# Attention beside a state-space convolution: 14 of 16 normalising multiplications on GpSimd, and two small transfers of the gate held back

## The chip, the cores and the metric

The kernel runs on one NeuronCore of a Trainium2 chip. The metric is the device time of one execution in microseconds, the median of several runs. The engines are TensorE (PE in the profile), VectorE (DVE), ScalarE (ACT), GpSimd (POOL) and SyncE (SP); GpSimd and SyncE issue most of the transfers.

## The reference

Two branches are computed from inputs of 2048 rows by 448 columns in bf16, and a gate mixes them.

```
g = sigmoid((x * gate_w).sum(-1))                  # one number per row
a = softmax(q k^T / sqrt(28)) v, then @ wo         # 16 heads of 28, one shared k and v
K[d, l] = Re sum_n C[d,n] exp(dt[d] A[d,n] l) dt[d] B[d,n]     # 256 modes, complex
b = causal convolution of u with K along the rows, rounded to bf16, + u * Dskip
out = g * a + (1 - g) * b                          # b is called with u = x
```

## The kernel before, in words

**Attention.** The 16 units are the four query chunks of 512 rows times the four groups of four heads. A unit has 64 score tiles (16 key tiles times four heads) of 128 x 512 in PSUM; 1024 tiles in all are taken in turn three and two at a time, as 410 sets. For each set TensorE multiplies `qT` or its copy `qM` with `kT` (L1422, L456, L1456; near the end L1444), ScalarE takes the exponential of the whole set in one instruction (L1497), and TensorE adds `expT` times `vaug` into `psB` (L1518). A column of ones in `vaug` gives the softmax's denominators.

At the end of each of the first 15 units, `norm(i)` does the following. VectorE copies `psB` to `acc` (L1210; `acc` has two halves, used in turn). GpSimd sends the denominators to the small tile `denT`. VectorE takes reciprocals (L1216) and, from unit 12 on, multiplies them by the gate (L1218). GpSimd sends them to the DRAM buffer `R_scratch` and reads them back, spread over partitions, into `rdenB` with four transfers. At last `onT = acc * rdenB` is computed: 128 x 512 elements, two f32 operands in SBUF, a bf16 result (L1222). The sixteenth unit has a path of its own (`scaled`). After units 3, 7 and 11, `outp` multiplies `onT` by `Wo` (L1190) and VectorE adds the result into `O` (L1201); the last chunk has `early` and `last`.

`qproj(i + 2)` prepares the query projections of a unit two units ahead, with VectorE's L933 and L939, and four transfers of GpSimd copy `qT` to `qM`.

**Convolution.** There are 14 blocks `c` of 32 channels. VectorE builds a table of powers for each: `masters` (L968 to L988), `tables` (L1025, L1040, L1044, L1048, L1054, L1058, and at its end the negation L1061). GpSimd contributes two small copies per block (L1011, L1013). TensorE turns a table into the convolution's kernel (`kgen`, L1084), VectorE copies this to `kstg` (L1096), transfers write it to `KP_scratch`, SyncE loads it back in Toeplitz form into ring buffers (`tload`), and TensorE convolves (`conv`, L1151), with VectorE's L1161 and L1181 at the end of each of 28 halves.

**The gate.** `g` is computed at the start into the tile `gt` (L769 to L773). Two transfers on GpSimd's queue then send 512 single f32 values to `RG_scratch` (`gw`, L774) and read them back in another layout (`gr`, L776), which L1218 needs in units 12 to 14.

**Order.** Nothing is written in final order. `Prog.op` and `Prog.dma` record operations with engine, estimated time, priority `pr` and dependences, and `schedule` plays them through: at each step it takes the operation that can start first, by (earliest start, `pr`, number). So every engine's order is fixed when the program is built, and an estimate that changes at one place moves instructions of all engines behind it. While it runs, each engine follows its order and waits on semaphores. One estimate belongs to GpSimd and VectorE together: a GpSimd operation of 500 ns or more is taken to hold VectorE up for `PORT` = 0.55 of its time (L356, L357). Where TensorE would be idle, the plan inserts a filler matmul (L1403).

Of the kernel before, what the change touches and what calls it, by code (L numbers as in the profile page):

```python
# [7 lines left out]
ALU = mybir.AluOpType  # L8
# [4 lines left out]
P = 128  # L13
# [29 lines left out]
XQ = NT * 512  # L43
QS = 4 * D + 64
GATE = (30, 35)
XDVE = ((1, 0), (1, 1), (1, 2))
WARM = 64
HELD = ((27, 3), (27, 9), (27, 15), (27, 21))
# [40 lines left out]
def dram(t, off, dims):  # L89
    return bass.AP(tensor=t.tensor, offset=t.offset + off, ap=[list(d) for d in dims])  # L90
# [7 lines left out]
class Prog:  # L98
# [101 lines left out]
    def schedule(self):  # L200
# [17 lines left out]
        free = {e: 0.0 for e in ENG}  # L218
# [18 lines left out]
        while done < n:  # L237
            best = None
            for e in ENG:
                T = free[e]  # L240
                for i in ready[e]:
                    o = ops[i]
                    r = max(rt[i], T)
                    if o.lock is not None:
# [3 lines left out]
                        r = max(r, L[1] + (300.0 if o.pr >= 2 else 0.0))  # L248
                    for k in o.comm or ():
                        if k in comm:  # L250
                            r = max(r, ops[comm[k]].end)
                    if o.psb == 3:
                        if not opened:
                            continue
                        for x in ready["pe"]:
                            if ops[x].pr <= 0.0 and r < rt[x] < r + o.ns - self.NEAR:
                                r = max(rt[x], T) + ops[x].ns
                    if e == "pe":
                        j = (npe + o.ni - self.FIRST - 1) // self.BLOCK + 1
                        if j < len(block):  # L260
                            r = max(r, block[j])
                            if o.pr >= 1 and block[-1] > r:
                                left = self.FIRST + (len(block) - 2) * self.BLOCK - npe - o.ni
                                r = max(r, block[-1] - left / self.NEED)
                    if o.slot is not None and o.slot[0] == "T" and self.spaced[0] < r < self.spaced[1]:
                        r = max(r, lastT + self.GAP)
# [5 lines left out]
            o = ops[i]  # L272
            spare = [x for x in locks if x[0] is None and x[1] <= free[e]]
            if e == "pe" and (opened or spare) and r > self.FWIN and self.filler is not None and npe > self.FIRST + self.BLOCK:
# [5 lines left out]
                if r - T >= w and busy < self.FLOW * self.FWIN and (j >= len(block) or block[j] <= T):  # L280
                    b = 6 if opened else spare[0][3]
                    o = self.op("pe", lambda x, b=b: self.filler(x, b), self.FILL, rd=["one", "id"], ni=2)
# [7 lines left out]
                    i, r = o.i, T  # L290
                    ready[e].append(i)
            ready[e].remove(i)
            if e == "pe" and o.mode != mode:
                r = max(r, free[e] + self.SWITCH)
# [35 lines left out]
            if o.slot is not None:  # L330
                free[e] = r + o.iss * o.ndma
                s = r if e == "pool" else max(r, dmafree)
                end = max(s + o.ns, free[e]) + self.DMA_NS + o.extra
                if e == "pool" and o.ns >= self.PUSHES:
                    for x in flight:
                        x[1] = max(x[1], r)
                        if x[2] > r:
                            x[2] += self.PUSH * o.ns
                            t = x[2] + self.DMA_NS + x[0].extra
                            if t > x[0].end:  # L340
                                x[0].end = t
                                for j in succ[x[0].i]:
                                    rt[j] = max(rt[j], t + self.SEM_NS + (self.LATE if ops[j].pr in self.LAZY and r < 360000.0 else 0.0))
                    flight = [x for x in flight if x[2] > r]
                if o.slot[0] == "T":
                    flight.append([o, s, max(s + o.ns, free[e])])
                if o.ns > 1000.0 and e == "sp":
                    self.moving = [x for x in self.moving if x[1] > r - 20000.0] + [(r, end)]
                dmafree = max(dmafree, s) + o.ns
            else:  # L350
                ns = o.ns
                if e == "pe" and self.HALF[0] < r < self.HALF[1]:
                    ns *= self.HALF[2]
                free[e] = r + ns
                end = free[e] + o.lat
                if e == "pool" and o.ns >= 500.0:  # L356
                    free["dve"] = max(free["dve"], r) + self.PORT * o.ns  # L357
            o.end = end
            if o.unlock is not None:
                L = [x for x in locks if x[0] is o.unlock][0]  # L360
# [88 lines left out]
def el(n, rate=0.96, fix=68):  # L449
    return fix + n / rate  # L450
# [23 lines left out]
class Kernel:  # L474
# [205 lines left out]
    def prep_x(self):  # L680
# [6 lines left out]
        for q in range(4):  # L687
            for hp in range(2):
# [14 lines left out]
                key = ("xT", hp, q)  # L703
                if (hp, q) not in XDVE:
                    pg.op("act", lambda e, d=dst, s=src: e.activation(d, s, AF.Copy), 1000, rd=[("b", b)], wr=[key])
# [498 lines left out]
    def norm(self, i):  # L1204
        pg = self.pg
        g = i % 4
        ao = 512 * (i % 2)
        av = self.acc.v(0, P, ao, [[1, 512]])
        ov = self.onT.v(0, P, 512 * g, [[1, 512]])
        pg.op("dve", lambda e: e.tensor_copy(av, self.psB.v(0, P, 0, [[1, 512]])), el(512), rd=[("b", 6)], wr=[("acc", i % 2)], pr=0)  # L1210
        dv = self.denT.v(0, P, 0, [[1, 16]])
        if True:
            rs = self.acc.rs
            pg.dma([(dv, bass.AP(tensor=self.acc.h, offset=28 * rs + ao, ap=[[32 * rs, 4], [16, 32], [1, 16]]))],
                   (128, 64), "dn", rd=[("acc", i % 2)], wr=["dn"], pr=0, eng="pool", extra=5000)
            pg.op("dve", lambda e: e.reciprocal(dv, dv), 163, rd=["dn"], wr=["dn"], pr=2)  # L1216
            if i >= 12:
                pg.op("dve", lambda e: e.tensor_tensor(dv, dv, self.gt.v(0, P, 32, [[1, 16]]), ALU.mult), 80, rd=["dn", "gT"], wr=["dn"], pr=2)  # L1218
            pg.dma([(dram(self.R, i * 2048, [[16, P], [1, 16]]), dv)], (128, 64), "rw", rd=["dn"], wr=[("R", i)], pr=0, eng="pool", extra=4500)
            pg.dma([(self.rdenB.v(32 * h, 32, 0, [[1, 512]]), dram(self.R, i * 2048 + 512 * h, [[0, 32], [1, 512]])) for h in range(4)],  # L1220
                   (128, 2048), "rdb", rd=[("R", i)], wr=["rd"], pr=0, eng="pool", extra=5500 if i < 14 else 1000)
            pg.op("dve", lambda e: e.tensor_tensor(ov, av, self.rdenB.v(0, P, 0, [[1, 512]]), ALU.mult),  # L1222
                  el(512), rd=[("acc", i % 2), "rd", "onw"], wr=[("on", g)], pr=2)

    def tailmats(self):
        pg = self.pg
# [148 lines left out]
    def main(self):  # L1375
        pg = self.pg
# [31 lines left out]
        def qk(s):  # L1408
# [42 lines left out]
            def full(e, t, b):  # L1451
                if t >= NLAST:
                    part(e, t, b, 0, False)
                    return part(e, t, b, 1, False)
                i, kt, h = dec(t)
                return e.matmul(self.psS.v(0, P, 512 * b, [[1, 512]]), kT.v(0, P, 128 * kt, [[1, 128]]),  # L1456
                                self.qM.v(0, P, (i % 2) * XQ + 512 * h, [[1, 512]]),
                                start=True, stop=True, tile_position=(0, 0), skip_group_check=True)
            if s < 8 or len(ts) == 3 or s >= 14 and (ts[0] % 64 < NEWQ or s >= ROWS):
                rd = set()  # L1460
                for t in ts:
                    i, kt, h = dec(t)
                    rd |= {("q", i % 2), ("kT", (kt if t < NLAST else declast(t)[1]) // 4)}
                o = pg.op("pe", row, 220, rd=sorted(rd, key=str), wr=bk, pr=0, mode="q", ni=2 * len(ts))
# [3 lines left out]
            else:  # L1468
                for t, b in zip(ts, bs):
                    i, kt, h = dec(t)  # L1470
                    kt = kt if t < NLAST else declast(t)[1]
                    o = pg.op("pe", lambda e, t=t, b=b: full(e, t, b), 220, rd=[("qM", i % 2), ("kT", kt // 4)],
                              wr=[("b", b)], pr=0, mode="f", ni=2)
            if s in GATE:
                pg.after[self.gate[GATE.index(s)]] = o.i
            if s < WARM and ts[0] % 64 < 52 and (ts[0] < 64 or ts[0] % 64 > 14):
# [16 lines left out]
            for t in ts:  # L1493
# [3 lines left out]
            o = pg.op("act", lambda e: e.activation(expT.v(0, P, 512 * es[0], spread(es, n)),  # L1497
                                                self.psS.v(0, P, 512 * bs[0], spread(bs, n)),
                                                AF.Exp, scale=SQ), 63.5 + 426.5 * n, rd=bk, wr=ew, pr=0)
            self.lastexp = o.i  # L1500

        def pv(v):
            ts = range(4 * v, 4 * v + 4)
# [35 lines left out]
        for s in range(len(sets)):  # L1539
            qk(s)  # L1540
            last = sets[s][-1]
            if s >= 2:
                while nv < NTL // 4 and 4 * nv + 3 <= sets[s - 2][-1]:
                    pv(nv)
                    nv += 1
                    if nv % 64 == 0 and nv // 64 < 4:
                        for tt in range(4):
                            self.outp(nv // 64 - 1, tt)
            for t in sets[s]:
                if t % 64 == 63 and t // 64 + 2 < 16:  # L1550
                    self.qproj(t // 64 + 2)
# [68 lines left out]
```

## Time and profile before

| | |
|---|---|
| median of 3 runs (range) | 496.68 us (496.52 to 496.79) |
| the profiled execution: its own time / span | 499.2 / 497.2 us |
| granted TensorE clock | 0.997 |
| VectorE's multiplication L1222 | 15 times, 682 ns each |
| GpSimd's copies L1011 / L1013 | 14 each, mean 1025 / 692 ns |
| `qM` transfers, median from issue to landing | 4.6 us |
| `RG_scratch` write / read back, issue to landing | 10.8 / 4.4 us |

The span goes from the first instruction to the last; the execution's own time is measured from outside and is 2.0 us longer. It lies 2.5 us over the median of the runs that were timed without a profile.

### The profile page before, as it was taken

Reading aid. Unit: us, or ns where it says so; the run is one execution under the profiler, and the core shown is the slowest. Engines: PE = TensorE matmul, PEld = TensorE weight load, DVE = VectorE, ACT = ScalarE, POOL = GpSimd, SP = SyncE. Lnnn points to the kernel's source line nnn. Section 1 sums busy time; section 2 is a strip of 40 time slices with the busy share of each in tenths; the row PEclk is TensorE's granted clock in tenths of the full one; section 3 lists DMA queues with packets and bytes.
Section 4 is the critical chain, followed back from the end, with each engine's and each line's share of the span. In section 5 each row is a group of like instructions: output and inputs, shape, how many; then the busy total and the mean of one; then the engine's idle time right before and its main releaser. Section 6 shows DMA issues by size and latency. Waiting matters only on the chain.

```text
span 497.2 us, 17393 instructions
## 1 busy us (share of the span) xinstructions
PE 476.1 (96%) x7657; PEld 218.4 (44%) x7657; DVE 456.3 (92%) x847; ACT 482.2 (97%) x433; POOL 220.4 (44%) x390
## 2 busy tenths in 40 slices
PE   8889999999999999999999999999999999999897
PEld 6423233353443435444443434444434354545443
DVE  6999999999999999999999999999999999993334
ACT  6989999999999999999999999999999999999995
POOL 8415034225243435767339376653764433431110
PEclk9989999999999999999999999999999999999999
DMA  8945012916719267873924956688393759595932
GB/s 254 269 57 112 1 34 57 343 45 178 229 18 337 69 188 219 227 211 94 309 68 100 323 163 139 179 227 205 114 238 112 225 145 290 196 279 159 284 105 70
DMA packets 91767, 85.44 MB, mean 172 GB/s; under 512 B 24970, under 2 KB 86716, under 8 KB 91692
## 3 DMA queue, kind: packets, MB, share of 16 engines
q1 hardware_dynamic: 80794, 72.49, 49.9%
q0 software_dynamic: 10624, 11.70, 10.6%
q8 instruction: 60, 0.98, 0.8%
q14 instruction: 15, 0.12, 0.1%
q10 hardware_dynamic: 274, 0.14, 0.1%
HBM read 76.36 MB, written 5.23 MB: 164 GB/s over the span
## 4 chain that ended last, share of the span: by engine, by line
DVE 55%; ACT 32%; PE 9%; DMA 2%; issue 1%; POOL 0%
ACT expT L1497 32%; DVE tab L1025 16%; DVE tab L1040 9%; DVE tab L1054 4%; DVE msq L968 3%; DVE tmp L1048 3%; DVE kstg L1096 2%; DMA qM<-qT 2%; DVE cst L1161 2%; DVE mbf L988 2%; DVE T L972 2%; DVE T L970 2%; DVE qT L933 1%; DVE qT L939 1%; DVE acc L1210 1%
## 5 line engine op out<-in xcount | busy, mean ns | idle before, releaser
L1497 ACT ACTIVATE expT<-psS 128x1536 bf16<-128x1536 f32 (+1 forms) x410 | 464.9, 1332 | 4.1 <-PE psS L1456 2.1
L1025 DVE TENSOR_TENSOR tab<-tab,mbf 128x512 bf16<-128x512 bf16 (+4 forms) x140 | 139.7, 1001 | 0.0
L456 PE MATMUL psS<-qT,kT 32*128 32x512 bf16 x713 | 101.2, 379 | 7.8 <-ACT expT L1497 4.9
L1518 PE MATMUL psB<-expT,vaug 128*32 128x512 bf16 x1000 | 100.2, 390 | 0.1
L170 POOL DMA_DIRECT2D KP_scratch<-kstg x104 | 57.9, 563 | 72.5 <-DVE kstg L1096 71.8
L1040 DVE TENSOR_TENSOR tab<-tab 128x256 bf16<-128x256 bf16 (+4 forms) x140 | 77.7, 575 | 0.0
L1456 PE MATMUL psS<-qM,kT 128*128 128x512 bf16 x240 | 72.8, 385 | 2.8 <-DMA qM<-qT 1.8
L1518 PEld LDWEIGHTS psB<-expT,vaug 128*32 128x32 bf16 x1000 | 25.6, 93 | 77.2 <-issue 72.6
L170 POOL DMA_DIRECT2D qM<-qT x64 | 32.6, 518 | 44.0 <-DVE qT L939 18.9
L170 POOL DMA_DIRECT2D U<-in_A_x_dram x60 | 39.7, 666 | 24.0 <-PE psS L1151 10.6
L1403 PE MATMUL psB<-ident,one 128*128 128x512 bf16 x155 | 49.4, 384 | 0.0
L1437 PEld LDWEIGHTS <-kT 32*128 32x128 bf16 x713 | 24.9, 91 | 47.4 <-issue 37.2
L170 POOL DMA_DIRECT2D rdenB<-R_scratch x60 | 30.6, 517 | 32.1 <-DMA R_scratch<-denT 32.0
L1151 PE MATMUL psX<-T,U 128*26 128x128 bf16 (+3 forms) x1792 | 42.8, 226 | 0.8 <-issue 0.8
L1151 PEld LDWEIGHTS psX<-T,U 128*26 128x26 bf16 (+3 forms) x1792 | 36.7, 138 | 14.1 <-issue 10.9
L1151 PE MATMUL psS<-T,U 128*26 128x128 bf16 (+3 forms) x1600 | 39.2, 227 | 0.9 <-issue 0.7
L1151 PEld LDWEIGHTS psS<-T,U 128*26 128x26 bf16 (+3 forms) x1600 | 32.4, 138 | 13.6 <-issue 10.0
L1054 DVE TENSOR_TENSOR tab<-tab,tmp 128x1984 bf16<-128x1984 bf16 x28 | 32.3, 1184 | 0.1
L1048 DVE TENSOR_TENSOR tmp<-tmp,mq 128x64 bf16<-128x64 bf16 (+4 forms) x70 | 25.6, 365 | 0.4
L968 DVE TENSOR_TENSOR msq<-T 128x512 f32<-128x512 f32 (+1 forms) x40 | 24.8, 620 | 0.0
L1456 PEld LDWEIGHTS psS<-qM,kT 128*128 128x128 bf16 x240 | 15.0, 98 | 21.1 <-ACT expT L1497 14.8
L170 POOL DMA_DIRECT2D R_scratch<-denT x15 | 8.6, 571 | 34.4 <-DVE denT L1216 14.0
(198 smaller groups left out, 543.2 us busy)
## 6 DMA issues: line engine op xcount, KB each, us to landing
T<-KP_scratch SPq DMA_DIRECT2D x212, 272.0 KB, 5.2
rdenB<-R_scratch POOLq DMA_DIRECT2D x60, 64.0 KB, 3.1
U<-KP_scratch SPq DMA_DIRECT2D x12, 272.0 KB, 5.5
U<-in_A_x_dram SPq DMA_DIRECT2D x20, 112.0 KB, 4.4
qM<-qT POOLq DMA_DIRECT2D x64, 32.0 KB, 4.6
tab<-in_A_x_dram SPq DMA_DIRECT2D x4, 448.0 KB, 5.4
KP_scratch<-kstg POOLq DMA_DIRECT2D x104, 16.0 KB, 2.4
xT<-XS_scratch POOLq DMA_DIRECT2D x3, 448.0 KB, 4.8
```

What stands on the lines that cost most here:

```text
L170: return [e.dma_start(o, i, **kw) for o, i in pairs]
L456: return e.add_instruction(mybir.InstMatmult(start_tensor_calc=True, stop_tensor_calc=True, tile_size=(32, 128), tile_position=pos, bass_s ...
L968: pg.op("dve", lambda e: e.tensor_tensor(m2(msq), z2, z2, ALU.mult), el(2 * n), rd=[kr, ki] + first, wr=["msq"], pr=pr)
L1025: mul = lambda e, o, a, b: e.tensor_tensor(o, a, b, ALU.mult)
L1040: vo(lambda e, dv=dv, tv=tv, k=k: e.tensor_tensor(dv, dv, tv, ALU.add if k else ALU.subtract), n, [kt[k], kd[k]], [kd[k]], 1.92 if lv else ...
L1048: vo(lambda e, w=w, lv=lv: e.tensor_tensor(rho.v(0, P, (32 - 2 * w) * 2, [[64, 32], [2, w], [1, 2]]), rho.v(0, P, (32 - w) * 2, [[64, 32], ...
L1054: vo(lambda e, k=k: e.tensor_tensor(tab.v(0, P, FM + k * FP + 2, [[64, 32], [2, 31], [1, 2]]), tab.v(0, P, lm + k * PL + 62, [[64, 32], [- ...
L1151: r = e.matmul(ps.v(32 * j, 32 - m0, 128 * k, [[1, 128]]), self.U.v(0, P, (4 * gi + j) % UA // UC * UW + (2 * m0 + par) * UC + (4 * gi + j ...
L1403: return e.matmul(t.v(0, P, off, [[1, 512]]), self.one.v(0, P, 2, [[0, P]]), self.ident.v(0, P, 0, [[0, 4], [1, P]]), start=b != 6, stop=b ...
L1456: return e.matmul(self.psS.v(0, P, 512 * b, [[1, 512]]), kT.v(0, P, 128 * kt, [[1, 128]]), self.qM.v(0, P, (i % 2) * XQ + 512 * h, [[1, 51 ...
L1497: o = pg.op("act", lambda e: e.activation(expT.v(0, P, 512 * es[0], spread(es, n)), self.psS.v(0, P, 512 * bs[0], spread(bs, n)), AF.Exp, ...
L1518: r = e.matmul(self.psB.v(32 * h, 32, 0, [[1, 512]]), vaug.v(0, P, 32 * kt, [[1, 32]]), expT.v(0, P, 512 * ring[t], [[1, 512]]), start=(kt ...
```

## The change

Three edits:

- In `norm`, the multiplication of units 0 to 13 is put on GpSimd instead of VectorE, with an estimate of 2200 ns and priority 2.1. Unit 14 stays on VectorE.
- In `schedule`, an operation with priority 2.1 is exempt from the `PORT` estimate: the plan takes it to cost VectorE nothing.
- In `main`, the first of the gate's transfers (`gw`) gets a dependence on the exponential of set 24 (counted from 0). The second one waits for the first, as before.

```diff
+GATEOUT = 24
...
                 if e == "pool" and o.ns >= 500.0:
-                    free["dve"] = max(free["dve"], r) + self.PORT * o.ns
+                    free["dve"] = max(free["dve"], r) + (0.0 if o.pr == 2.1 else self.PORT * o.ns)
...
-            pg.op("dve", lambda e: e.tensor_tensor(ov, av, self.rdenB.v(0, P, 0, [[1, 512]]), ALU.mult),
-                  el(512), rd=[("acc", i % 2), "rd", "onw"], wr=[("on", g)], pr=2)
+            far = i < 14
+            pg.op("pool" if far else "dve", lambda e: e.tensor_tensor(ov, av, self.rdenB.v(0, P, 0, [[1, 512]]), ALU.mult),
+                  2200.0 if far else el(512), rd=[("acc", i % 2), "rd", "onw"], wr=[("on", g)], pr=2.1 if far else 2)
...
             self.lastexp = o.i
+            if s == GATEOUT:
+                self.gw.deps[o.i] = 1
```

The instructions themselves stay the same in kind and number, apart from the engine of the 14 multiplications and from fillers, of which the new order has 8 more (170 instead of 162). ScalarE's order is unchanged. The orders of TensorE and VectorE are the same up to the first multiplication, near 85 us, and differ from there on.

## The prediction

> **What bounds the kernel now.** I read the page first (busy shares, slices, the chain), then the idle gaps of ScalarE, then the stages, and last the places where VectorE and GpSimd meet. Busy time, and the costliest groups of ScalarE and VectorE:
>
> ```profile
> PE 476.1 (96%) x7657; PEld 218.4 (44%) x7657; DVE 456.3 (92%) x847; ACT 482.2 (97%) x433; POOL 220.4 (44%) x390
> ...
> DVE 55%; ACT 32%; PE 9%; DMA 2%; issue 1%; POOL 0%
> ...
> L1497 ACT ACTIVATE expT<-psS 128x1536 bf16<-128x1536 f32 (+1 forms) x410 | 464.9, 1332 | 4.1 <-PE psS L1456 2.1
> ```
>
> ScalarE's 410 exponentials (L1497) run nearly end to end from 21.8 to 490.75 us and stood idle only 4.1 us before one of them. That is all that a faster supply could win in the stream. Yet the chain runs 55% over VectorE: ScalarE is only just the slower of two.
>
> The stages show the second one:
>
> ```profile
> 150.00:200.00 50.00, 49.26 (x796) 22.04 (x794) 50.00 (x88) 50.00 (x45) 22.31 (x39) 1.00 0.65 199
> 250.00:300.00 50.00, 48.65 (x697) 20.59 (x694) 50.00 (x85) 49.91 (x45) 31.16 (x50) 1.00 0.60 162
> 350.00:400.00 50.00, 47.60 (x821) 21.26 (x817) 50.00 (x91) 50.00 (x46) 26.07 (x46) 1.00 0.68 187
> 450.00:498.00 48.00, 41.97 (x925) 22.69 (x923) 15.04 (x30) 41.22 (x38) 5.22 (x10) 1.00 0.48 145
> ```
>
> (busy us of PE, PEld, DVE, ACT, POOL, then clock, DMA share, GB/s.) VectorE has no free moment until about 457 us, when its fourteenth table is done, and then almost nothing. So VectorE's work up to that table has a delivery date. TensorE takes each table in a fixed place of its order (L1084), after the negation L1061. In the timeline that handover leaves 0.2 to 0.8 us in nine of 14 tables and 1.26 us in the last (450.49 to 451.75), and TensorE waits for almost none of them.
>
> The largest gaps of ScalarE are at the start:
>
> ```profile
> 34.22 1.02 ACT L1497 ACTIVATE expT<-psS 128x1024 bf16<-128x1024 f32 x1 [1.30 <-PE psS L1456]
> 36.05 1.45 ACT L1497 ACTIVATE expT<-psS 128x1536 bf16<-128x1536 f32 x1 [0.81 <-PE psS L1422]
> ...
> 24.99 0.79 POOL L170 DMA_DIRECT2D RG_scratch<-gt  x1 [1.22 <-DVE gt L772]
> 27.54 0.30 POOL L1011 COPY tab<-mbf 128x128 bf16<-128x128 bf16 x1 [1.76 <-DVE mbf L988]
> 36.12 0.71 POOL L170 DMA_DIRECT2D gt<-RG_scratch  x1 [8.29 <-DMA RG_scratch<-gt]
> ```
>
> Four gaps between 32.91 and 38.90 us sum to 1.30 + 0.81 + 0.19 + 0.18 = 2.5 us. TensorE waits 1.8 us for the copy qM, which takes 10.1 us to land where the next takes 2.7. In those microseconds the gate's 512 four-byte elements are under way (landing in 10.8 us), and SP's issues of U, mostly 0.63 us, stretch to 4.80 us at 29.11.
>
> **The change, part by part.** *Gate transfers.* They leave the first 36 us and wait for exponential 24 (start 52.36 us, so about 53.9). Behind the first of them on GpSimd's queue stand denT of unit 0 (sent at 56.63 before), then the second transfer, then qM of unit 2, sent at 66.10 and first needed at tile 128, near 84 us. Even a landing of 10.8 us again ends at about 66, so this costs nothing; without that cover a late qM would cost its lateness. At the start the gain lies between 0 (the jam is U's own) and 2.5 us. I take 2.5, because jam and transfer coincide.
>
> *Off VectorE.* A multiplication L1222 takes 682 ns, 0.60 from its start to the next start. Thirteen stand before the last negation (the thirteenth at 435.9, the fourteenth at 462.7): 13 x 0.60 = 7.8 us. In the new order one qT cast (0.60) and the two small denT operations (0.24 + 0.18) also come later and one O addition (0.41) earlier, 0.6 us net. So VectorE has 8.4 us less to do before the last table.
>
> *What the order asks for.* The built program counts on that. The plan is told that these 14 cost VectorE nothing while they run, and places TensorE's table multiplications earlier among the score tiles: table 13 behind tile 923 instead of 943, table 10 behind 765 instead of 783. A tile is 464.9 / 1024 = 0.454 us of ScalarE, so table 13 is due 20 x 0.454 = 9.1 us sooner. VectorE may be late by the handover of 1.26 less the smallest one seen, 0.19 (table 3), and ScalarE has one prepared set left (1.02 us). Lateness that ScalarE feels: 9.1 - 8.4 - 1.07 - 1.02 = -1.4 us, plus 13 p, where p is the time that one multiplication on GpSimd takes from VectorE. Table 10 gives 8.2 - (11 x 0.60 + 3 x 0.60) - (0.64 - 0.19) - 1.02 = -1.7 us, plus 11 p: table 13 decides. The start's 2.5 us don't add to this, since they move ScalarE and not VectorE: the change is the larger of -2.5 us (ScalarE's pace) and -1.4 + 13 p (VectorE's).
>
> *The price p.* No row shows a GpSimd operation with two inputs. The nearest are the 28 small copies:
>
> ```profile
> 341.55 0.69 DVE L1061 TENSOR_SCALAR tab<-tab 128x2048 bf16<-128x2048 bf16 x1
> 341.70 0.74 POOL L1013 COPY tab<-seedw 128x128 bf16<-128x128 bf16 x1 [4.59 <-DVE seedw L984]
> 342.15 0.78 DVE L968 TENSOR_TENSOR msq<-T 128x512 f32<-128x512 f32 x1
> ...
> 351.06 1.27 POOL L1013 COPY tab<-seedw 128x128 bf16<-128x128 bf16 x1
> 351.10 0.40 DVE L972 TENSOR_TENSOR T<-msq 128x256 f32<-128x256 f32 x1
> 351.43 0.41 DVE L1025 TENSOR_TENSOR tab<-tab,mbf 128x512 bf16<-128x512 bf16 x1
> 351.76 0.41 DVE L988 CAST mbf<-T 128x512 bf16<-128x512 f32 x1
> 352.10 0.67 DVE L933 TENSOR_REDUCE qT<-psX 128x512 bf16<-128x512 f32 x1
> ```
>
> A copy that meets a VectorE operation reading PSUM takes 0.29 to 0.31 us; one that meets table work waits. At 351.06 it sat through three SBUF operations and ended with the fourth, which reads PSUM. Of 15 copies over 0.5 us, nine ended in a PSUM reader, two in a tiny copy, and four at the border of two table operations. Those four stretched VectorE's next operation by about 0.09 us (L968: 0.78 against a mean of 0.687). So the two engines exclude each other, and VectorE pays for GpSimd's reads. The multiplication reads 2 x 512 elements where the copy read 128: 8 x 0.09 = 0.7 us. From above: memsets of 128 and 448 elements take 0.20 and 0.48 us, 0.85 ns per element; two reads and a write of 512 make 1.3 us. From below: 0, if it always fits under PSUM readers. It begins under a PSUM reader (0.68 us) nine times in 15, which covers about half a microsecond. With a hold of 0.7: (4 x 0.7 + 9 x 0.25 + 2 x 0.5) / 15 = 0.40; with 1.1: (4 x 1.1 + 9 x 0.6 + 2 x 0.9) / 15 = 0.77. I take the middle, p = 0.55; ends 0 and 1.3. There is no reason for p below zero.
>
> The Trainium skill (SBUF — State Buffer, Who interferes with whom) says that a VectorE instruction with two SBUF inputs contends with a GpSimd instruction that reads SBUF, and that whoever issues first keeps the shared port for its whole instruction; the rows above agree, and the rule speaks against this change. The skill's GPSIMD Engine Reference (Performance versus the Vector engine) gives 4497 ns for 2048 fp32 elements of tensor_tensor; a quarter is 1.12 us, an estimate, and with it as the hold the sum would come to about +8.9 us (p = 0.79 by the same weights).
>
> *Sum.* -1.4 + 13 x 0.55 = +5.8 us. The profiled execution took 499.2 us (span 497.2, 2.0 around it), 2.5 above the median of 496.68: 505.0 there, 502.5 as a median. A measurement of this kernel tells about 0.2%, 1 us, from no change.
>
> **The rivals.** *Faster: the multiplications hide under PSUM readers* (p up to 0.03). For it: VectorE spends some 90 us in them, and most copies got in there. Against: four copies entered between table operations, and the multiplication is longer than any PSUM reader by the nearest prices. Then VectorE's pace gives -1.4 us and the start yields 1.4 of its 2.5: 495.3, at best 494.2 if TensorE's lead is larger. It decides below p = 0.11, where the sum crosses zero.
>
> *No change*: p between 0.03 and 0.18, VectorE's gain just used up by the tighter order: 495.7 to 497.7. If nothing is won at the start this case keeps its place, since VectorE's pace decides it.
>
> *The hold is over 1.0 us in VectorE's terms*: -1.4 + 13 x 1.05 and more, from 509 up.
>
> *GpSimd starves and its queue is late.* Behind a multiplication stand denT, qM and the KP writes; one copy at 36.84 us took 4.99 us, through ten VectorE operations into the eleventh. TensorE's output multiplications L1190 need units 3, 7 and 11. A 5 us wait less 1 us of lead costs up to 4 us at each, 4 to 12 beyond VectorE's -1.4: 499 to 507.
>
> **How the numbers follow.** Forecast (p from 0.18 to 1.0, 497.7 to 508.3) 0.53, hidden 0.18, no change 0.09, long hold 0.10, starved queue 0.10. The range 495.0 to 508.5 leaves out the long hold and the best of the hidden case. Faster 0.18, same 0.09, slower 0.73.
>
> **What would show it.** Right: VectorE operations beside a GpSimd L1222 stretched by 0.3 to 1 us; ScalarE's gaps at 33 to 39 us gone; new gaps behind table multiplications, growing towards 450 us, with TensorE waiting for L1061 or what stands before it; VectorE done with table 13 near 450, not 442. Wrong: VectorE's operations at their old lengths and table 13 by 443; or the gaps at 33 to 39 still there; or ScalarE waiting on output multiplications instead.

## The result, and the profile after

The changed kernel took 512.55 us, the median of 4 runs (508.67 to 516.65), against 496.69 us (496.52 to 496.79). The four times follow the granted TensorE clock (508.67 us at 1.000, 510.56 at 0.997, 514.54 at 0.990, 516.65 at 0.976), and the ratio leaves out the last of them. The other three have a median of 510.56 us: slower by 2.7%, ratio 1.027 with a 95% interval of 1.0223 to 1.0318. The profiled execution took 510.56 us, its span 508.6 us.

The page of the changed kernel (its code stands one to four lines lower than that of before, so L1497 is now L1499 and the multiplication L1222 is L1224):

```profile
PE 476.9 (94%) x7665; PEld 217.3 (43%) x7665; DVE 461.0 (91%) x833; ACT 484.1 (95%) x433; POOL 243.5 (48%) x404
...
DVE 73%; ACT 16%; PE 6%; POOL 2%; issue 1%
...
L1499 ACT ACTIVATE expT<-psS 128x1536 bf16<-128x1536 f32 (+1 forms) x410 | 466.8, 1306 | 13.6 <-PE psS L457 9.9
...
L1224 POOL TENSOR_TENSOR onT<-acc,rdenB 128x512 bf16<-128x512 f32 x14 | 24.4, 1742 | 5.5 <-DMA rdenB<-R_scratch 5.3
```

VectorE has 14 operations less and is busy for longer: 461.0 us against 456.3. The chain now runs 73% over VectorE (55% before), and ScalarE waits 13.6 us before its exponentials instead of 4.1.

Where those waits lie, from ScalarE's timeline of the changed kernel, the start and one place of the middle:

```profile
23.43 37.46 ACT L1499 ACTIVATE expT<-psS 128x1024 bf16<-128x1024 f32 x33
```

```profile
239.99 1.02 ACT L1499 ACTIVATE expT<-psS 128x1024 bf16<-128x1024 f32 x1 [1.82 <-PE psS L1458]
241.37 1.45 ACT L1499 ACTIVATE expT<-psS 128x1536 bf16<-128x1536 f32 x1 [0.36 <-PE psS L457]
```

The gaps at 33 to 39 us are gone. In their place some twenty gaps of up to 1.8 us stand between 101 and 448 us. ScalarE waits for TensorE there, and TensorE waits for VectorE; the waits of TensorE in the changed kernel (who waited for whom: total, times, longest):

```profile
PE psS L1173 <- DVE cst L1162: 4.7, 5, 2.6
PE psS L457 <- ACT expT L1499: 3.3, 14, 0.5
PE psX L1173 <- DVE cst L1162: 2.4, 3, 1.1
...
PE psX L1085 <- DVE tab L1062: 1.5, 2, 1.3
...
PE psX L1085 <- DVE kstg L1097: 1.1, 1, 1.1
```

Only a part is the wait for a table (L1085 for L1062). More often TensorE met the lateness earlier, at the end of a convolution half, where it needs VectorE's product with the gate (L1162). (The 3.3 us for ScalarE are no part of the lateness; they were 4.9 before.) The place at 240 us shows what such a wait can bring with it: TensorE had waited 2.63 us there, its granted clock was then 0.50 from 240.28 to 243.69 us, and a score multiplication took 0.60 to 0.63 us in that time instead of 0.38.

What makes VectorE late is seen beside GpSimd's multiplications. Two of the fourteen in the changed kernel's timeline (start, duration):

```profile
294.55 0.69 DVE L1211 COPY acc<-psB 128x512 f32<-128x512 f32 x1
294.93 1.29 POOL L1224 TENSOR_TENSOR onT<-acc,rdenB 128x512 bf16<-128x512 f32 x1
295.15 3.23 DVE L1026 TENSOR_TENSOR tab<-tab,mbf 128x4096 bf16<-128x4096 bf16 x1
```

```profile
174.01 0.69 DVE L1211 COPY acc<-psB 128x512 f32<-128x512 f32 x1
174.38 1.29 POOL L1224 TENSOR_TENSOR onT<-acc,rdenB 128x512 bf16<-128x512 f32 x1
174.62 0.68 DVE L934 TENSOR_REDUCE qT<-psS 128x512 bf16<-128x512 f32 x1
175.21 0.68 DVE L1162 TENSOR_TENSOR cst<-psX,omq 128x512 bf16<-128x512 f32 x1
```

At 295 us a table operation of 2.28 us takes 3.23: it stood still for 0.95 us. At 174 us three readers of PSUM follow each other and nothing is lost. A multiplication that GpSimd can start at once takes 1.27 to 1.31 us; the mean of 1742 ns holds waiting.

### The profile page after: what moved, and what is told of

The parts are those of the page before. It is cut to its first block, busy times and chain, and to the rows that moved or that the text cites. A ratio compares the mean times of both kernels' runs of the same rounds, so it can differ in the third digit from the quotient of the medians.

```text
span 508.6 us, 17435 instructions
## 1 busy us (share of the span) xinstructions
PE 476.9 (94%) x7665; PEld 217.3 (43%) x7665; DVE 461.0 (91%) x833; ACT 484.1 (95%) x433; POOL 243.5 (48%) x404
## 4 chain that ended last, share of the span: by engine, by line
DVE 73%; ACT 16%; PE 6%; POOL 2%; issue 1%
DVE tab L1026 21%; ACT expT L1499 15%; DVE tab L1041 10%; DVE tab L1055 5%; DVE msq L969 5%; DVE tmp L1049 3%; DVE T L971 3%; DVE kstg L1097 3%; DVE mbf L989 2%; DVE cst L1162 2%; DVE T L973 2%; DVE qT L940 2%; DVE qT L934 2%; DVE tab L1062 1%; DVE acc L1211 1%
## 5 line engine op out<-in xcount | busy, mean ns | idle before, releaser
L1499 ACT ACTIVATE expT<-psS 128x1536 bf16<-128x1536 f32 (+1 forms) x410 | 466.8, 1306 | 13.6 <-PE psS L457 9.9
L1026 DVE TENSOR_TENSOR tab<-tab,mbf 128x512 bf16<-128x512 bf16 (+4 forms) x140 | 144.0, 1030 | 0.0
L1405 PE MATMUL psB<-ident,one 128*128 128x512 bf16 x158 | 51.4, 389 | 0.0
L1152 PE MATMUL psS<-T,U 128*26 128x128 bf16 (+3 forms) x1728 | 40.4, 226 | 1.2 <-issue 1.2
L1152 PEld LDWEIGHTS psS<-T,U 128*26 128x26 bf16 (+3 forms) x1728 | 34.5, 138 | 13.8 <-issue 10.3
L1152 PE MATMUL psX<-T,U 128*26 128x128 bf16 (+3 forms) x1664 | 39.3, 227 | 0.1
L1152 PEld LDWEIGHTS psX<-T,U 128*26 128x26 bf16 (+3 forms) x1664 | 33.1, 139 | 12.8 <-issue 9.8
L1049 DVE TENSOR_TENSOR tmp<-tmp,mq 128x64 bf16<-128x64 bf16 (+4 forms) x70 | 27.4, 392 | 0.3
L969 DVE TENSOR_TENSOR msq<-T 128x512 f32<-128x512 f32 (+1 forms) x40 | 27.7, 692 | 0.0
L1224 POOL TENSOR_TENSOR onT<-acc,rdenB 128x512 bf16<-128x512 f32 x14 | 24.4, 1742 | 5.5 <-DMA rdenB<-R_scratch 5.3
L171 POOL DMA_DIRECT2D denT<-acc x15 | 10.8, 719 | 29.9 <-DVE acc L1211 27.7
```

Source lines behind the costliest of these rows:

```text
L171: return [e.dma_start(o, i, **kw) for o, i in pairs]
L969: pg.op("dve", lambda e: e.tensor_tensor(m2(msq), z2, z2, ALU.mult), el(2 * n), rd=[kr, ki] + first, wr=["msq"], pr=pr)
L1026: mul = lambda e, o, a, b: e.tensor_tensor(o, a, b, ALU.mult)
L1049: vo(lambda e, w=w, lv=lv: e.tensor_tensor(rho.v(0, P, (32 - 2 * w) * 2, [[64, 32], [2, w], [1, 2]]), rho.v(0, P, (32 - w) * 2, [[64, 32], ...
L1152: r = e.matmul(ps.v(32 * j, 32 - m0, 128 * k, [[1, 128]]), self.U.v(0, P, (4 * gi + j) % UA // UC * UW + (2 * m0 + par) * UC + (4 * gi + j ...
L1405: return e.matmul(t.v(0, P, off, [[1, 512]]), self.one.v(0, P, 2, [[0, P]]), self.ident.v(0, P, 0, [[0, 4], [1, P]]), start=b != 6, stop=b ...
```

## The experiments

In the later sessions the kernel before ran at 497.5 to 497.8 us in the median, with single runs from 495.9 up; each ratio below is against the runs of before on the same chip.

**The gate's transfers alone** (kernel before with the third edit):

```diff
+GATEOUT = 24
...
+            if s == GATEOUT:
+                self.gw.deps[o.i] = 1
```

> The kernel before with the third edit alone (the gate's transfers wait for exponential 24); all multiplications stay on VectorE. Theory A (the jam at 28 to 37 us is the gate's): ScalarE's gaps at 33 to 39 us (2.5 us) go; VectorE, which is not moved, gives at most about 1 us handover and one set of lead (1.0 us) back, so 1.0 to 2.5 us faster: 494.2 to 495.7. Theory B (the jam is that of the U loads): the gaps stay, 496.7. Theory C (VectorE's pace swallows all of it): the gaps at the start go, and others of the same sum come behind the tables: 496.2 to 496.7.

Measured: ratio 0.9991 (0.9969 to 1.0013), no difference. SP's issues of the U loads, the kernel before first and then this one:

```profile
15.62 23.98 SPq L170 DMA_DIRECT2D U<-in_A_x_dram  x20
```

```profile
14.52 17.94 SPq L171 DMA_DIRECT2D U<-in_A_x_dram  x20
```

So the jam is the gate's: without its 512 small elements in the way the same 20 issues take 6 us less. In the seven profiled executions with the early transfers they take 22.8 to 24.8 us, in the five with the late ones 17.3 to 18.4. But the kernel is not faster. The next two runs bear on why.

**The multiplications alone** (changed kernel without the third edit):

```diff
-            if s == GATEOUT:
-                self.gw.deps[o.i] = 1
```

> The changed kernel without the third edit: 14 multiplications on GpSimd and the plan's exemption, the gate's transfers early again. Theory A (VectorE's pace decides, ScalarE's start is swallowed): the time of the changed kernel, profiled near 510, within 1.5 us; gaps at 33 to 39 us are back and the later ones sum to 2.5 us less. Theory B (the start counts in full): 2.5 us slower than the changed kernel.

Measured: 513.18 us, ratio 1.030 (1.0255 to 1.0344), an interval that overlaps that of the changed kernel. The loss comes with the multiplications and does not need the third edit. Between the two theories the time does not decide: the profiled execution took 513.11 us, 2.6 more than that of the changed kernel, as B says and outside the 1.5 us of A. But B's reason is not there. The gaps at 33 to 39 us did not come back although the gate's transfers were early again, which A had wrong as well: TensorE waited for none of the first qM copies (the trace has no landing for the four of unit 0; those of unit 1 landed in at most 2.9 us). Instead the granted clock was 0.50 twice in this execution, from 210.37 to 213.78 and from 241.09 to 247.91 us, against once in the changed kernel.

**The kernel before, profiled again.**

> The kernel before, unchanged, for a second profile. Theory A (the late copy qM at the start belonged to the one profiled execution, in which the gate's jam happened to hold it): qM of unit 0 lands in 2 to 4 us, no ScalarE gaps at 33 to 39 us, time 496 to 498; the U issues of SP still take about 24 us, as in the kernels with the early gate transfers. Theory B (the late qM is in every execution, and the gate-only kernel lost its gain elsewhere): 10 us, the 2.5 us of gaps again.

Measured: 497.30 us, span 495.6. ScalarE's timeline of this second profile:

```profile
23.50 37.46 ACT L1497 ACTIVATE expT<-psS 128x1024 bf16<-128x1024 f32 x33
```

No gap up to 60 us, and qM lands in 2.0 to 4.8 us, while SP's issues of U still take 22.8 us. So the late qM is not in every execution, and its 2.5 us of gaps are as large as what the first profiled execution (499.2) lay over the median. Nor is it in that one alone. The kernel with copies further below has the early gate transfers too, and in its profiled execution (504.09 us, 3.7 over its median) the last qM of unit 0 landed in 11.2 us:

```profile
35.52 1.02 ACT L1499 ACTIVATE expT<-psS 128x1024 bf16<-128x1024 f32 x1 [2.75 <-PE psS L1458]
37.36 1.45 ACT L1499 ACTIVATE expT<-psS 128x1536 bf16<-128x1536 f32 x1 [0.81 <-PE psS L1424]
```

It came late in two of seven profiled executions with the early transfers and in none of five with the late ones. Whether the third edit prevents it is not shown by so few. In both late cases the granted clock was 0.50 as well (33.95 to 37.36 us in the first profile, 33.28 to 40.11 here), so the gaps are TensorE's wait for qM (1.79 and 3.25 us) and slower matmuls around it.

**The same order, but GpSimd reads nothing** (the 14 multiplications are left out and memsets of the same places stand for them):

```diff
-            pg.op("pool" if far else "dve", lambda e: e.tensor_tensor(ov, av, self.rdenB..., ALU.mult),
+            pg.op("pool" if far else "dve", lambda e: e.memset(ov, 0.0) if far else e.tensor_tensor(ov, av, self.rdenB..., ALU.mult),
```

> The changed kernel with its order as it is, in which GpSimd's 14 operations are memsets of the same places: they read nothing, and the 14 multiplications are left out of the computation. Theory A (the loss needs GpSimd's reads; p = 0 for an operation that only writes): the change's own sum with p = 0, -1.4 us, 495 to 497. Theory B (the order, the later placed transfers or GpSimd's queue lose the time by themselves): 503 or more.

Measured: ratio 1.0003 (0.9973 to 1.0033); the profiled execution took 495.47 us, 1.8 less than the second profile of before. This is the run that decides. Every place in every order is that of the changed kernel, and the loss is gone. Its page:

```profile
PE 475.4 (96%) x7665; PEld 216.5 (44%) x7665; DVE 447.5 (91%) x833; ACT 482.2 (98%) x433; POOL 230.1 (47%) x404
...
L1499 ACT ACTIVATE expT<-psS 128x1536 bf16<-128x1536 f32 (+1 forms) x410 | 464.8, 1328 | 0.9 <-PE psS L457 0.5
```

VectorE is busy 447.5 us here and 461.0 in the changed kernel with the same 833 operations in the same order: 13.5 us more. All of it lies before the end of table 13 (the changed kernel first; the second number is VectorE's busy time):

```profile
0.00:453.76 453.76, 446.45 (x804) 1.00 0.61 174
```

```profile
0.00:438.40 438.40, 432.96 (x804) 1.00 0.64 180
```

So 13.5 us belong to the 13 multiplications up to there, p = 1.04, and the fourteenth, behind the last table, cost nothing. Set side by side, the operations of VectorE beside 11 of the 13 are 12.8 us longer than in this kernel. The end of table 13 and TensorE's first multiplication with it, this kernel first and then the changed one:

```profile
437.70 0.69 DVE L1062 TENSOR_SCALAR tab<-tab 128x2048 bf16<-128x2048 bf16 x1
...
439.43 0.66 PE L1085 MATMUL psX<-tab 128*64 128x128 bf16 x16
```

```profile
453.07 0.69 DVE L1062 TENSOR_SCALAR tab<-tab 128x2048 bf16<-128x2048 bf16 x1
...
454.95 0.66 PE L1085 MATMUL psX<-tab 128*64 128x128 bf16 x16
```

From there to the last exponential it is 47.6 us in this kernel and 47.2 in the changed one, against 39.0 in the kernel before: the 20 tiles that the order moved behind this table. The difference in time between the two kernels lies before it.

**The multiplications once more** (kernel before; GpSimd repeats 11 of them after VectorE):

```diff
+            if i < 14 and g < 3:
+                pg.op("pool", lambda e: e.tensor_tensor(ov, av, self.rdenB.v(0, P, 0, [[1, 512]]), ALU.mult),
+                      2200.0, rd=[("acc", i % 2), "rd"], wr=[("on", g)], pr=2.1)
```

(with the plan's exemption for priority 2.1)

> The kernel before, in which GpSimd repeats 11 of VectorE's multiplications (units 0 to 13 but 3, 7 and 11) into the same place after VectorE; the plan counts nothing for it, table 13 stands behind tile 940. VectorE keeps all its work, so the time shows p alone: 11 p + 1.4 - 2.1. Theory A with p = 0.9: +9.2 us, 506; with p = 0.55: +5.4 us, 502; VectorE's operations beside the repeats longer by 0.7 to 1.1 us. Theory B (no contest for a port, the changed kernel lost its time by order and queue only): 496.7 within 1.

Measured: 507.02 us, ratio 1.0176 (1.0123 to 1.0228), +8.8 us. VectorE's busy time is 466.7 us against 456.7 in the second profile of before: 10.0 us for 11, 0.91 each on average. Here no work was taken from VectorE and the order is nearly that of before, so the price is seen alone. One of them:

```profile
239.53 1.28 POOL L1225 TENSOR_TENSOR onT<-acc,rdenB 128x512 bf16<-128x512 f32 x1
239.84 1.26 DVE L988 CAST mbf<-T 128x512 bf16<-128x512 f32 x1
```

A cast with one SBUF operand (0.42 us elsewhere) is held up as well.

**One operand, and none** (kernel before; GpSimd first puts a copy, or a memset, of 128 x 512 into the place that VectorE's multiplication then overwrites, 11 times; the plan counts nothing):

```diff
+            if i < 14 and g < 3:
+                pg.op("pool", lambda e: e.tensor_copy(ov, av), 2200.0, rd=[("acc", i % 2), "onw"], wr=[("on", g)], pr=2.1)
```

In the second kernel the operation is `e.memset(ov, 0.0)`.

> The kernel before, in which GpSimd makes 11 copies of 128 x 512 f32 to bf16 (one operand read) into the place that VectorE's multiplication then overwrites; the plan counts nothing for them, table 13 at tile 943 as before. Theory A (VectorE pays for what GpSimd reads): VectorE's operations beside them are longer by about half of what the multiplication costs, 0.3 to 0.6 us each; 11 x 0.45 - 2.1 = +2.9 us, +1 to +5. Theory B (only two-operand instructions exclude each other): 0.

> As the kernel with copies, with 11 memsets of 128 x 512 bf16 by GpSimd instead (no operand read), same order. Theory A (VectorE pays for reads): VectorE's two-operand operations beside them keep their lengths, 0 us within 1. Theory B (any GpSimd operation takes the port for its whole length): each takes about 0.4 us, +1 to +3 us.

Measured: copies 1.0064 (1.0034 to 1.0095), memsets 0.9983 (0.9954 to 1.0012). The same place in both timelines, with copies first:

```profile
322.40 0.62 POOL L1223 CAST onT<-acc 128x512 bf16<-128x512 f32 x1
322.50 1.09 DVE L1224 TENSOR_TENSOR onT<-acc,rdenB 128x512 bf16<-128x512 f32 x1
```

```profile
315.97 0.55 POOL L1223 MEMSET onT<- 128x512 bf16 x1
316.06 0.68 DVE L1224 TENSOR_TENSOR onT<-acc,rdenB 128x512 bf16<-128x512 f32 x1
```

Beside this copy VectorE's operation takes 1.09 us, 0.41 more than beside the memset. Six of the 11 copies stretched nothing; over all 11 VectorE is busy for 458.8 us against 456.2 with memsets, 0.24 us for each. No operation beside any of the 11 memsets was longer than usual. The two kernels have the same order, and a copy is little longer than a memset (0.62 against 0.54 us when it starts at once), so it is reading that costs: 0.24 us on average for one operand of 512, 0.9 to 1.0 us for two.

**What the plan should count.** Two kernels give the plan a price for each multiplication, instead of none:

```diff
-                    free["dve"] = max(free["dve"], r) + (0.0 if o.pr == 2.1 else self.PORT * o.ns)
+                    free["dve"] = max(free["dve"], r) + (el(512) if o.pr == 2.1 else self.PORT * o.ns)
```

In the other the line stays as before, and PORT gives 1210 ns.

> The changed kernel, but the plan counts 0.6 us of VectorE for each of the 14 multiplications on GpSimd instead of nothing, so that TensorE takes table 13 behind tile 940 (before 943, changed 923). Theory A (each multiplication takes p from VectorE, and the order asked for 9.1 us too much): with p = 0.9, as the date of table 13 in the changed kernel gives, 3 tiles x 0.454 - 8.1 + 13 x 0.9 - 2.1 = +2.9 us, 499.6 (498.5 to 501). With p = 0.55, as predicted, it would be no slower than before. Theory B (lateness of GpSimd's own queue and of the output multiplications stalls TensorE): as the changed kernel, 507 to 513.

> The changed kernel without the plan's exemption: each of the 14 multiplications on GpSimd counts 0.55 x 2200 = 1210 ns of VectorE, and TensorE takes table 13 behind tile 950 (before 943, changed 923). Theory A (VectorE's pace: p near 0.95 and the order's demand): -7 x 0.454 - 8.1 + 13 x 0.95 - 2.1 = -1.0, so ScalarE's pace decides, and what the plan adds at the end decides the rest: 496 to 499, no faster than before by more than 1 us. Theory B (the multiplications stall through GpSimd's queue, whatever the plan counts): 502 or more, as with 0.6 us counted.

Measured: with 0.6 us counted 502.65 us, ratio 1.0091 (1.0061 to 1.0121), +4.5 us; with 1.21 us 505.56 us, ratio 1.0182 (1.0117 to 1.0247). The first goes the way of the sum: the order asks for 7.7 us less (17 tiles), and two thirds of the loss go with it. But it lies over the range of theory A (498.5 to 501; +2.9 us expected), and what the rest is was not settled. The second misses: I expected 496 to 499, and 502 or more was theory B's. Its tables wait for TensorE (table 2 by 7.0 us, table 6 by 5.4, table 9 by 5.9, where the kernel before leaves 0.6, 3.9 and 1.2), so VectorE is not what is late there, and yet ScalarE has gaps before its exponentials at 145 to 148, at 256 and at 265 us. Nor did TensorE wait for GpSimd there, as theory B has it. Before 256 and 265 us it was busy with other matmuls (L1152 and L1085 above all) for 2.6 and 2.4 us between one score tile and the next, so this order puts too much between two sets; at 145 to 148 us the granted clock was 0.50 (143.17 to 146.58). How much of the loss that explains was not settled. What both show is that neither price given to the plan brought this offload back to the time before.

**Write-only work on GpSimd** (kernel before; VectorE's 14 copies of constants become 28 GpSimd memsets):

```diff
-        vo(lambda e: e.tensor_copy(tab.v(0, P, FM, [[FP, 2], [64, 32], [1, 2]]), self.one..., 128, ["one"], fk)
...
+        for k in range(2):
+            po(lambda e, k=k: e.memset(tab.v(0, P, FM + k * FP, [[64, 32], [1, 2]]), 1.0 - k), 70, done, [("F1", k)])
```

> The kernel before, with the 14 VectorE copies of constants into the tables (0.2 us each) replaced by 28 GpSimd memsets, which read nothing. Theory A (write-only work on GpSimd costs VectorE nothing): VectorE has 14 x 0.2 = 2.8 us less to do, its operations keep their lengths, and table 13 stands 3 tiles earlier; ScalarE's gaps behind tables (about 1.3 us in the stream) can go: 0 to 1.5 us faster. Theory B (GpSimd's memsets come late for TensorE, since its queue is in order): 1 to 5 us slower.

Measured: ratio 1.0059 (1.0045 to 1.0072), 2.9 us slower. VectorE's busy time fell by 1.4 us only (455.3 against 456.7), and TensorE's order changed with the plan. That is a miss: I expected 0 to 1.5 us faster, and theory B's 1 to 5 us slower is what came, though its reason is not seen: TensorE's waits in this kernel name no operation of GpSimd. That the memsets are free for VectorE does not make the reordered kernel faster; which of its moves costs the time stays open. No kernel here beats the one before.

## Why the prediction was wrong, point by point

**What bounds the kernel** was right. VectorE's work up to table 13 sets the pace, which the memset kernel shows: with VectorE's 13.5 us gone, the loss is gone. Of the 1.07 us of handover that the sum allowed it at table 13, only 0.1 to 0.3 show there: TensorE takes that table 1.19 us after VectorE's end in the changed kernel, 1.26 and 1.45 in the two profiles of before. TensorE had met the lateness earlier, at L1173.

**What the order asks for** was right, and the largest term that could be read before any run: 9.1 us forecast, 8.2 to 8.6 measured between table 13 and the last exponential. With p = 0 the sum gave -1.4 us; the kernel with memsets, which has p = 0 in that order, gave -1.8 by its profile and no difference by its timed runs.

**The price p** was the mis-sized term, and the step that failed: 0.55 forecast, 1.04 measured for the 13 multiplications that stand before table 13. Two steps led there. The hold was scaled from the 128-element copies to 0.7 and, from above, 1.1 us; it is 1.28 us, which the ladder of the memsets (0.85 ns per element, 1.3 us) had right and which I kept only as the end of the range. And the cover under PSUM readers was taken as half a microsecond in nine of 15 cases. In the changed kernel four of 14 multiplications began under a PSUM reader, and the multiplications are twice as long as such a reader and come when table work follows: all but three stretched what stood beside them, and only those three, which found PSUM readers or nothing around them, cost nothing. (The middle of the two weighted values, 0.40 and 0.77, is also 0.585 and not 0.55; that is 0.4 us of the sum.) The terms of the sum beside what the changed kernel's profile and the second profile of before show (the work taken off from the memset kernel; the demand is the 47.2 us from TensorE's first use of table 13 to the last exponential less the 39.0 of before, and the 0.3 us less are the handover's):

| us | forecast | measured |
|---|---|---|
| order's demand, less the lateness allowed | 9.1 - 2.1 = 7.0 | 8.2 - 0.3 = 7.9 |
| work taken off VectorE up to table 13 | -8.4 | -9.1 |
| 13 p | 7.2 | 13.5 |
| more idle time of VectorE before table 13 | 0 | 0.7 |
| end of the last exponential | +5.8 | +13.0 |

The price alone is 6.3 of the 7.2 us that were missing.

**The gain at the start** was wrong. That the gate's transfers jam the queue is shown, but the late qM, from which I took 2.5 us, is in some executions only, and the runs of the kernel with the third edit alone are no faster. The rows of one execution could not show this. The hint was there: that execution lay just 2.5 us over the median. Wrong, too, is that these 2.5 us "move ScalarE and not VectorE". In that execution VectorE was not without a free moment: it stood idle for 2.5 us between 25 us and the end of its first table, 0.3 us in the second profile, and ended that table at 74.74 instead of 72.37 us and table 13 at 450.49 instead of 448.67.

**From the profile to the median** I subtracted those 2.5 us. Since VectorE had lost most of them as well (2.4 us at the first table, 1.8 at the last), that was right to within a microsecond, though not for the reason given. With the measured p the forecast would have been 502.5 + 13 x (1.04 - 0.55) = 508.9 us, against the 510.56 us on which the ratio rests. That it comes so near is partly luck, since the other terms of the table miss by up to 0.9 us each and partly cancel.

**The rivals.** What came is the one with a hold of over 1.0 us in VectorE's terms, priced at 509 up with a chance of 0.10. Table 13 came 15.4 us later than with memsets; 0.5 us of that is the later first exponential, 13.5 are VectorE's stretched operations and the rest is idle time. The hidden case fell with the first stretched operation. The starved queue did not come about: TensorE waited only 1.0 us for GpSimd's L1224 in all.

**The Trainium skill.** The rule on the shared port (SBUF — State Buffer, Who interferes with whom) held: only GpSimd operations that read SBUF held VectorE up, the memsets did not. That the port is kept for the whole instruction agrees with the rows above to about 0.1 us: VectorE's operation at 295.15 us lost 0.95 of the 1.07 us that GpSimd's multiplication had still to run, and the one at 322.50 us 0.41 of the 0.52 us that were left of the copy. It does not account for the three places, listed at the end, where VectorE lost more than a whole multiplication.

## What to carry to other kernels

Before work is moved from a full VectorE to GpSimd, count what GpSimd reads: a multiplication of two 128 x 512 f32 operands saved 0.60 us and cost 1.04, a memset cost nothing. If a planner orders the engines, an operation that it takes for free is paid twice, since other engines are then told to be ready sooner. And before a gap is booked as a gain, look whether the profiled execution is itself slower than the median by as much, and profile the same kernel a second time.

## What the runs showed of the hardware that was not expected

- GpSimd's multiplication of 128 x 512 (two f32 operands, bf16 result) takes 1.27 to 1.31 us when it starts at once, a copy 0.62, a memset 0.54; on average they cost VectorE 0.9 to 1.0, 0.24 and 0 us.
- At 116, 235 and 261 us of the changed kernel VectorE lost 1.8, 2.2 and 1.8 us beside one multiplication of 1.3 to 1.4 us, more than its whole length. The stretch begins there before the multiplication, while GpSimd issues a transfer; in the kernel with memsets the same VectorE operations beside the same issues keep their lengths. Why stays open.
- One-operand casts of VectorE from SBUF (L988: 1.26 us instead of 0.42) are held up as two-operand operations are.
- A transfer of 512 separate 4-byte elements to DRAM landed in 9 to 11 us, even at a quiet time (9.3 us at 51 us in the changed kernel), and in the busy start it stretched 20 other issues from 17 to 18 us to 23 to 25.
- After TensorE had waited (1.79 us for qM in the first profile of before, 2.63 us for L1162 in the changed kernel) its granted clock was 0.50 for 3.41 us, from 33.95 and 240.28 us on. In the second profile of before it was 1.00 throughout up to 490 us.
